# The down products of a SwiGLU block: 26 products of 256 columns replaced by 49 products of 128

## The chip, the cores and the metric

The kernel runs on one core of one Trainium2 chip. Its time is the device time of one execution in microseconds (us). A core has five engines with instruction streams of their own: PE (TensorE, the matmuls; its weight loads are shown apart as PEld), DVE (VectorE), ACT (ScalarE), POOL (GpSimd) and SP (SyncE, which here only issues transfers). PE reads its operands from SBUF, the on-chip memory of 128 partitions, and writes PSUM, in banks of 128x512 f32 values. Data moves between SBUF and DRAM by DMA.

## The reference

Two blocks follow each other, everything in f32:

```
attention, for 8 batches x 8 heads, 576 positions, 64 wide:
    ret = (q @ k.T) / 8 * decay(head)        # lower triangle, gamma ** distance
    x   = ret @ v                            # bridged to 4608 tokens x 512
feed-forward:
    g   = x @ w_gate                         # 512 -> 1536
    val = x @ w_val                          # 512 -> 1536
    out = (silu(g) * val) @ w_out            # 1536 -> 512
```

The weights arrive as 64-bit values and are rounded to f32 on the chip.

## The kernel before, in words

**Tiles and stages.** The 4608 tokens are worked through as a first tile of 512 and four tiles of 1024 (in the code `n` = 1 to 4). Each tile has an up stage (gate and value) and a down stage (the product with w_out). The first tile is plain: `up0` and `down0` use 512-column matmuls, and while they run the attention of the first heads is computed and the weights are rounded (by ACT and DVE). From then on the attention of the head pairs that a later tile needs is spread as small pieces ("ticks" and `pieces`) between the matmuls of the tile before; `go_on(3)` places three such pieces behind a product of a down stage.

**The instruction streams.** The order on each engine is the order in which the program emits instructions (a manual schedule); `later(at, f)`, tables of slots and `merge` decide it. Waits on semaphores are added where data or a buffer is needed.

**Up stages** of the 1024-token tiles use a seven-product scheme (Strassen's, in a variant with fewer sums) at two levels. Weight sums for it come from DRAM (`up_sets`, written during tile 1), sums of x are made on POOL and DVE. The matmuls are those of L1183 with 256 moving columns; results are read from PSUM on DVE and ACT (L1040, L1197), and POOL multiplies silu by val into `hid` (L1198).

**Down stages before.** `hid` holds 4 hidden groups x 4 token blocks of 256 tokens, each with 3 pieces of 128 hidden features (`qd`), so one operand is 128 x 3 x 256 = 128x768 values. The output has two halves of 256 columns. The plain form would need 4 x 4 x 2 = 32 block products; the table `DOWN` needs 26. Each of its lines names the PSUM accumulator, the operand slot, the operand sums made just before ("hops", in place in `hid` and in four more slots `hsum`), and the readings of the accumulator into eight partial results `part`. A product is 3 x 2 f32 matmuls (L1378); each f32 matmul is two passes on PE, so 12 passes of 256 moving columns. In `down_step` the hops go to POOL in one step of three (L886), else to DVE (L886, or L881 for a negated sum). An accumulator is read as 128x512 on DVE (L1040) or copied by ACT; sums of partial results without an accumulator are on POOL (L1040). Four PSUM banks are used in rotation.

**Weight sums of the down stages.** While the first tile's last up steps and its `down0` run, `out_sums` makes the sums of w_out that `DOWN` needs (`OUT_SUMS`): for `qd` 0 and 1 on POOL, for `qd` 2 on DVE (L886, 128x256). ACT first negates four blocks (`negate`, L916) so that POOL needs no negated sums. Each operand is stored to DRAM (`dn_ops`, 26 of 128x768) by SP's queue in 78 transfers of 128 KB. In the down stages `fetch` brings them back into a ring of eight places of 128x768, through ACT's queue and, for some, SP's. The first tile's outputs are copied from PSUM by ACT into `part[4:8]` (`out0`, L869), which the weight sums of `qd` 2 also use, and stored from there.

**The last steps of a down stage** also hold sums of x for the next tile's up stage (`x_first`, on POOL and DVE).

Of the kernel before, what the change touches and what calls it, by code (L numbers as in the profile page):

```python
# [22 lines left out]
def tables(gamma, scale, L):  # L23
# [27 lines left out]
DOWN = [  # L51
    "0= | 1: sub 16 1 11 | copy 0",
    "1= | 11: add 3 3 2, add 3 3 11, sub 17 7 3 | copy 1",
    "2= | 2: nad 3 3 15 | copy 2",
    "1+ | 16: nad 7 7 16 | copy 3",
    "3= | 17: sub 18 0 17 | sub 3 3 b",
    "2+ | 3: add 11 11 8, nad 11 11 9 | add 1 b 1",
    "0+ | 7: sub 9 5 9, sub 1 1 9, sub 13 13 1 | sub 3 3 b",
    "3+ | 18: sub 19 8 13, sub 12 12 19, add 0 0 2 | copy 4",
    "1+ | 11: add 16 4 12, add 3 6 16 | copy 5",  # L60
    "2= | 13: sub 16 17 16 | sub 2 b 2",
    "3+ | 0: nad 9 15 0 | sub 6 2 b",
    "0= | 3:  | copy 7",
    "1= | 16: add 12 12 0 | sub 7 7 b",
    "3+ | 9:  | add 1 b 1, neg 7 1",
    "2+ | 5: add 13 13 10 | copy 8",
    "1+ | 12:  | sub 6 6 b",
    "0= | 19:  | sub 6 6 b, out 4 6",
    "2= | 13: sub 7 1 10 | sub 2 b 2, sub 2 2 7",
    "3+ | 15: add 3 3 14, nad 3 3 15 | add 3 b 3, out 3 3",  # L70
    "1= | 6: add 8 8 1 | sub 7 b 7",
    "2+ | 7:  | copy 9",
    "3+ | 3: sub 14 14 13 | add 9 b 9",
    "0+ | 8: add 4 4 6, sub 4 8 4 | add 5 b 5, sub 0 0 5, sub 8 5 8, out 5 8",
    "2+ | 10:  | add 0 b 0, sub 7 b 7, out 1 0, sub 4 4 7, sub 9 7 9, out 2 9",
    "3+ | 14:  | add 2 b 2, out 6 2",
    "0+ | 4:  | add 4 b 4, out 0 4",
]
OUT_SUMS = [
    "14 | 10: add 8 4 5, add 9 2 3, nad 10 8 9",  # L80
    "2 | 11: add 11 0 1",
    "9 | 5: ",
    "19 | 9: neg 9 9",
    "15 | 12: sub 12 3 7",
    "0 | 11: sub 11 11 8",
    "1 | 13: sub 13 1 5",
    "6 | 10: add 10 0 2",
    "3 | 12: add 9 2 8, sub 12 1 9",
    "22 | 9: add 9 9 7",
    "4 | 11: sub 11 0 3",  # L90
    "11 | 13: nad 13 3 6",
    "7 | 0: ",
    "25 | 10: sub 10 6 2",
    "20 | 8: add 12 6 7, add 8 8 12",
    "23 | 4: ",
    "16 | 9: nad 9 5 7",
    "8 | 11: add 11 2 4",
    "5 | 13: add 13 1 3",
    "18 | 10: sub 10 12 13",
    "10 | 8: sub 13 7 13, sub 8 13 0",  # L100
    "17 | 9: add 9 5 12",
    "24 | 12: ",
    "12 | 3: ",
    "13 | 13: ",
    "21 | 6: ",
]


# [4 lines left out]
def terms(text):  # L113

    return [t.split() for t in text.split(",") if t.strip()]


def lines(table):

    r = []  # L120
    for line in table:
        f = [s.strip() for s in line.split("|")]
        e = [int(f[0][0]), f[0][1] == "="]
        for s in f[1:-1]:
            slot, ops = s.split(":")
            e += [int(slot), terms(ops)]
        r.append(e + [terms(f[-1])])
    return r
# [3 lines left out]
def kernel(  # L132
# [37 lines left out]
    P = 128  # L170
# [59 lines left out]
    hsum = rest[:, dn_at + 4096 : dn_at + 4096 + 3072].rearrange("p (s q x) -> p s q x", s=4, q=NQ)  # L230
# [636 lines left out]
    def out0():  # L867
        for i, (bank, o) in enumerate(zip(banks, part[4:8], strict=True)):
            nc.scalar.copy(out=o, in_=bank)  # L869
            nc.sync.dma_start(out=out[i * P : (i + 1) * P, :], in_=o)  # L870


    down = lines(DOWN)
    N = len(down)

    def add(eng, op, view, to=None):
        dst, srcs = view(int(op[1])) if to is None else to, [view(int(a)) for a in op[2:]]
        if op[0] == "neg":
            eng.tensor_scalar(out=dst, in0=srcs[0], scalar1=-1.0, scalar2=None, op0=ALU.mult)
        elif op[0] == "nad" and eng is nc.vector:  # L880
            eng.scalar_tensor_tensor(out=dst, in0=srcs[0], scalar=-1.0, in1=srcs[1], op0=ALU.mult, op1=ALU.subtract)  # L881
        elif op[0] == "nad":
            eng.tensor_tensor(out=dst, in0=srcs[0], in1=srcs[1], op=ALU.add)
            eng.tensor_scalar(out=dst, in0=dst, scalar1=-1.0, scalar2=None, op0=ALU.mult)
        else:
            eng.tensor_tensor(out=dst, in0=srcs[0], in1=srcs[1], op=ALU.add if op[0] == "add" else ALU.subtract)  # L886

    up_sets = [[dr.tile([P, 1792], F32, name=f"up{qd}_{o}") for o in SETS] for qd in range(NQ)]
    dn_ops = [dr.tile([P, 768], F32, name=f"dn{i}") for i in range(N)]
# [6 lines left out]
    vector_places = x0_places + more_places[6:] + [rest[:, part_at + TB * i : part_at + TB * (i + 1)] for i in range(8)]  # L896

    def events_of(text):
        r = []
        for line in text:  # L900
            i, s = line.split("|")
            slot, ops = s.split(":")
            r += [(int(op[1]), op) for op in terms(ops)] + [(None, int(slot), int(i))]
        return r

    swaps = {"add 9 2 3, nad 10 8 9": "sub 9 14 2, sub 10 9 8", "neg 9 9": "", "nad 13 3 6": "sub 13 14 6", "nad 9 5 7": "sub 9 15 7"}
    signed = list(OUT_SUMS)
    for old, new in swaps.items():
        at = [i for i, line in enumerate(signed) if old in line]
        assert len(at) == 1  # L910
        signed[at[0]] = signed[at[0]].replace(old, new)
    negatives = [x_odd[:, r, 640 : 640 + TB] for r in (2, 3)] + more_places[4:6]

    def negate(qd):
        for n, s in enumerate((3, 5)):
            nc.scalar.mul(out=negatives[2 * qd + n], in_=w_dn[:, qd, s // 2, s % 2], mul=-1.0)  # L916

    def out_sums(qd):


        place = {}

        def free(p):
            if not any(p is q for q in x0_places):
                sum_places.append(p)

        eng, sum_places = (nc.vector, vector_places) if qd + 1 == NQ else (nc.gpsimd, pool_places)
        events = events_of(OUT_SUMS if qd + 1 == NQ else signed)

        def view(s):  # L930
            if s > 13:
                return negatives[2 * qd + s - 14]
            return w_dn[:, qd, s // 2, s % 2] if s < 8 else place[s]

        def used(e):
            return [e[1]] if e[0] is None else [int(a) for a in e[1][2:]]

        def release(k):

            for s in list(place):  # L940
                for e in events[k + 1 :]:
                    if s in used(e):
                        break
                    if s == e[0]:
                        free(place.pop(s))
                        break
                else:
                    free(place.pop(s))

        def do(k):  # L950
            e = events[k]
            if e[0] is None:
                _, slot, i = e
                nc.sync.dma_start(out=dn_ops[i][:, qd * TB : (qd + 1) * TB], in_=view(slot))
            else:
                new = sum_places.pop(0)
# [605 lines left out]
```

## Time and profile before

Three runs took 1024.98, 1025.04 and 1025.64 us (median 1025.04). The profile is that of one execution of 1026.62 us, whose span on the core is 1024.9 us; 1.7 us lie around the span.

| | busy, us | share of the span |
|---|---|---|
| PE | 1003.7 | 98% |
| PEld | 823.0 | 80% |
| DVE | 713.3 | 70% |
| POOL | 557.5 | 54% |
| ACT | 286.3 | 28% |

The four down stages lie at 328.7 to 406.0, 547.6 to 622.6, 757.5 to 826.8 and 953.6 to 1021.1 us of the span, 289.1 us together. The first holds the most attention work, the last none. The granted clock of TensorE is 1.00 in all four.

How to read the lines: a line of the timeline is start, duration (us), engine, code line, operation, output<-inputs, shapes and a count when several of one kind ran in a row; in square brackets stands how long the engine had been idle and what ended it. A line of the groups ends with the busy time, the mean of one in ns, and the idle time before them. Names like bankB are PSUM banks; arena, rest and io are parts of SBUF; dn is the DRAM copy of the down weight sums.

### The profile page before, as it was taken

Reading aid. Unit: us, or ns where it says so; the run is one execution under the profiler, and the core shown is the slowest. Engines: PE = TensorE matmul, PEld = TensorE weight load, DVE = VectorE, ACT = ScalarE, POOL = GpSimd, SP = SyncE. Lnnn points to the kernel's source line nnn. Section 1 sums busy time; section 2 is a strip of 40 time slices with the busy share of each in tenths; the row PEclk is TensorE's granted clock in tenths of the full one; section 3 lists DMA queues with packets and bytes.
Section 4 is the critical chain, followed back from the end, with each engine's and each line's share of the span. In section 5 each row is a group of like instructions: output and inputs, shape, how many; then the busy total and the mean of one; then the engine's idle time right before and its main releaser. Section 6 shows DMA issues by size and latency. Waiting matters only on the chain.

```text
span 1024.9 us, 21387 instructions
## 1 busy us (share of the span) xinstructions
PE 1003.7 (98%) x8336; PEld 823.0 (80%) x8336; DVE 713.3 (70%) x1215; ACT 286.3 (28%) x638; POOL 557.5 (54%) x602
## 2 busy tenths in 40 slices
PE   6999989899999999999999999999999999999998
PEld 5654545788888888888888888888888888888887
DVE  5488877588787766876778688848585767566644
ACT  4465531122332411132332111133320012232110
POOL 3400178997563208665656247755582486566515
PEclk9999999999999999999999999999999999999999
DMA  9999877966496897656658767444455454445552
GB/s 244 253 272 239 202 203 247 275 202 176 120 266 157 221 238 225 194 157 174 187 181 225 195 186 210 148 141 144 157 193 155 144 185 154 143 147 188 175 161 100
DMA packets 281612, 194.38 MB, mean 190 GB/s; under 512 B 212968, under 2 KB 251112, under 8 KB 281512
## 3 DMA queue, kind: packets, MB, share of 16 engines
q1 hardware_dynamic: 247112, 93.52, 35.6%
q10 hardware_dynamic: 33760, 99.10, 29.5%
q8 instruction: 66, 1.08, 0.4%
q0 software_dynamic: 640, 0.39, 0.2%
q14 instruction: 34, 0.28, 0.1%
HBM read 154.04 MB, written 38.93 MB: 188 GB/s over the span
## 4 chain that ended last, share of the span: by engine, by line
PE 69%; DVE 2%; issue 1%; SPq 0%; DMA 0%; DVEq 0%; ACT 0%
PE bankC L1183 9%; PE bankB L1183 9%; PE bankA L1183 9%; PE bankE L1183 9%; PE bankB L1378 7%; PE bankE L1378 7%; PE bankC L1378 7%; PE bankA L1378 6%; PE outer L1183 2%; PE inner L1183 2%; DVE rest L1040 2%; PE outer L532 1%; PE outer L559 1%; PE inner L573 1%; PE inner L543 1%
## 5 line engine op out<-in xcount | busy, mean ns | idle before, releaser
L1040 POOL TENSOR_TENSOR rest<-rest 128x512 f32<-128x512 f32 (+1 forms) x141 | 150.3, 1077 | 156.1 <-DVE rest L1040 114.1
L1198 POOL TENSOR_TENSOR arena<-rest,io 128x256 f32<-128x256 f32 x156 | 113.8, 740 | 88.6 <-ACT io L1197 83.2
L1197 ACT ACTIVATE io<-rest 128x256 f32<-128x256 f32 x192 | 79.4, 417 | 212.0 <-DVE rest L1040 149.6
L1183 PE MATMUL bankB<-rest,arena 128*128 128x256 f32 x448 | 114.9, 381 | 1.0 <-DVE rest L1040 0.9
L1040 DVE TENSOR_TENSOR rest<-bankB,rest 128x512 f32<-128x512 f32 x116 | 78.5, 685 | 47.7 <-PE bankB L1183 32.2
L1183 PE MATMUL bankA<-rest,arena 128*128 128x256 f32 x412 | 105.4, 381 | 1.4 <-POOL rest L1040 0.9
L1183 PE MATMUL bankC<-rest,arena 128*128 128x256 f32 x416 | 106.4, 380 | 0.4 <-DVE rest L1040 0.2
L1040 DVE TENSOR_TENSOR rest<-bankA,rest 128x512 f32<-128x512 f32 x110 | 74.5, 684 | 45.9 <-PE bankA L1183 21.3
L1040 DVE TENSOR_TENSOR rest<-bankC,rest 128x512 f32<-128x512 f32 x110 | 74.7, 685 | 32.0 <-PE bankC L1183 18.9
L1183 PEld LDWEIGHTS bankB<-rest,arena 128*128 128x128 f32 x448 | 84.5, 190 | 13.8 <-POOL rest L1040 1.2
L1183 PE MATMUL bankE<-rest,arena 128*128 128x256 f32 x372 | 95.0, 380 | 0.4 <-DVE rest L1040 0.3
L1040 DVE TENSOR_TENSOR rest<-bankE,rest 128x512 f32<-128x512 f32 x106 | 71.8, 685 | 31.3 <-PE bankE L1183 14.8
L1183 PEld LDWEIGHTS bankA<-rest,arena 128*128 128x128 f32 x412 | 77.7, 190 | 13.6 <-DVE rest L1040 1.8
L1183 PEld LDWEIGHTS bankC<-rest,arena 128*128 128x128 f32 x416 | 78.3, 190 | 12.6 <-DVE rest L1040 1.4
L1040 POOL TENSOR_TENSOR arena<-arena 128x256 f32<-128x256 f32 (+1 forms) x80 | 74.4, 953 | 12.1 <-DMA up<-arena 6.2
L1183 PEld LDWEIGHTS bankE<-rest,arena 128*128 128x128 f32 x372 | 69.9, 190 | 11.7 <-DVE rest L1040 1.6
L886 POOL TENSOR_TENSOR rest<-rest 128x256 f32<-128x256 f32 x43 | 33.4, 800 | 53.8 <-DVE rest L407 36.6
L1378 PE MATMUL bankB<-arena 128*128 128x256 f32 x264 | 61.0, 381 | 0.0
L1378 PE MATMUL bankE<-arena 128*128 128x256 f32 x264 | 60.8, 380 | 0.0
L1378 PEld LDWEIGHTS bankE<-arena 128*128 128x128 f32 x264 | 49.9, 190 | 6.9
L1378 PEld LDWEIGHTS bankB<-arena 128*128 128x128 f32 x264 | 49.8, 190 | 6.9
L886 POOL TENSOR_TENSOR arena<-arena 128x768 f32<-128x768 f32 x24 | 47.0, 1961 | 15.3 <-DVE arena L1198 14.7
(267 smaller groups left out, 1881.1 us busy)
## 6 DMA issues: line engine op xcount, KB each, us to landing
arena<-up ACTq DMA_DIRECT2D x63, 896.0 KB, 4.6
arena<-dn ACTq DMA_DIRECT2D x65, 384.0 KB, 3.5
arena<-dn SPq DMA_DIRECT2D x39, 384.0 KB, 3.2
dn<-rest SPq DMA_DIRECT2D x78, 128.0 KB, 2.0
out_dram<-rest SPq DMA_DIRECT2D x35, 256.0 KB, 3.1
qk<-in_q_dram SPq DMA_DIRECT2D x108, 72.0 KB, 3.1
qk<-in_k_dram SPq DMA_DIRECT2D x108, 72.0 KB, 3.1
up<-arena SPq DMA_DIRECT2D x14, 512.0 KB, 2.9
```

The lines of the kernel that those rows point to most:

```text
L532: m = nc.tensor.matmul(value(i, hl, c), s["v"][rows, at], ret[rows, c % 2 if whole(i) else hl, c // 2], start=start, stop=start, skip_grou ...
L543: nc.tensor.matmul(z[half[hl], r, c], s["kn"][chunk(i, hl, 2 * c + r)], s["v"][rows, at], start=True, stop=True, skip_group_check=True)
L559: nc.tensor.matmul(xr[half[hl]] if c + 1 == NC else value(i, hl, c), state[half[hl], c, :], s["qT"][half[hl], ts(c, L)], start=False, stop ...
L573: nc.tensor.matmul(sc[chunk(i, hl, 2 * c + r)[0], r if whole(i) else hl, c], kT[half[hl], at], qT[half[hl], at], start=True, stop=True, sk ...
L886: eng.tensor_tensor(out=dst, in0=srcs[0], in1=srcs[1], op=ALU.add if op[0] == "add" else ALU.subtract)
L1040: eng.tensor_tensor(out=out, in0=a, in1=b, op=ALU.add if sign > 0 else ALU.subtract)
L1183: m = nc.tensor.matmul(b[:, g * TB : (g + 1) * TB], w[:, g], x, start=(opens and g == 0), stop=True, skip_group_check=True)
L1197: nc.scalar.activation(out=s, in_=src[:, 0:TB], func=AF.Silu)
L1198: (nc.vector if busy and o != 2 else nc.gpsimd).tensor_tensor(out=hid[:, qd, 2 * H + h, 2 * T + t], in0=src[:, TB : 2 * TB], in1=s, op=ALU ...
L1378: nc.tensor.matmul(b[:, m * TB : (m + 1) * TB], lhs[:, qd, ts(m, P)], w[:, qd], start=(opens and qd == 0 and m == 0), stop=(qd == NQ - 1), ...
```

## The change

The change replaces the down stages of the four 1024-token tiles and the weight sums that feed them; the up stages, the attention and the first tile's matmuls stay.

- **Products.** The down product is cut into 4 token blocks x 4 hidden groups x 4 output quarters of 128 columns, 64 plain block products, and the seven-product scheme is used at two levels, which needs 49. `DOWN_SETS` gives the seven outer products, `down_slots` the order of the 49 slots; the last two products of a set (7 and 4) are woven into the next set. A slot is 2 x 3 f32 matmuls, 12 passes of 128 moving columns. An accumulator is 128x256, still four banks in rotation.
- **Operand sums** (`down_sums`). The outer sums combine whole blocks of `hid`: 16 of 128x768 on DVE per tile, at slots 1, 3, 5, 7 (set 5), 8 to 11 (set 7), 14 to 17 (set 6) and 24 to 27 (set 3). The inner sums are four for each of seven sets, 28 of 128x768 on POOL per tile: the first three of set 1 are put into the last slots of the up stage, the fourth at slot 0, the others at slots 1-4, 6-9, 13-16, 20-23, 27-30 and 34-37. Before, a tile had 18 sums on DVE and 10 on POOL.
- **Readings** (`read`, `takes`). Accumulators are read as 128x256: 55 on DVE and 8 copies on ACT in each tile; sets 6 and 5 are read twice. POOL has two 128x512 sums (`closed`).
- **Fetches.** A transfer of 128x768 now holds two products' operands: 24 of 384 KB and one of 192 KB a tile, in the same ring, and `go_on(1 + s % 2)` places three attention pieces per two slots.
- **Weight sums** (`sums_of_w`, `out_sums`). 44 sums of 128x256 on POOL (`qd` 0 and 1 together) and 44 of 128x128 on DVE (`qd` 2); 80 stores of them and 9 of unchanged blocks (`raw_stores`) on SP's queue. The negations on ACT are gone. `out0` copies into `hid0[0]`, `hid0[2]` and the two halves of `io` instead of `part[4:8]`.
- **The rest.** `x_first` has its sums every other slot over the last 10 or 18 slots, and the four ticks of tile 1 are put in front of slots 4, 14, 26 and 38.

```diff
+DOWN_SETS = (1, 2, 4, 7, 6, 5, 3)
+def down_slots():
+    slots, begins = [], []
+    for k in range(len(DOWN_SETS)):
+        begins.append(len(slots))
+        own = [(k, i) for i in (1, 5, 2, 6, 3)]
+        if k:
+            own[1:1], own[5:5] = [(k - 1, 7)], [(k - 1, 4)]
+        slots += own
+    return slots + [(k, 7), (k, 4)], begins
+def sums_of_w():
+    r = []
+    def inner(o):
+        z = lambda k, m: (o, k, m)
+        t = lambda j: (o, j)
+        kept = [(o, 1, z(0, 0)), (o, 2, z(1, 0)), (o, 3, z(1, 1))] if o > 3 else []
+        r.append([(t(1), z(0, 1), z(0, 0)), (t(3), z(1, 1), z(0, 1)), (t(2), z(1, 1), t(1)), (t(4), z(1, 0), t(2)), *kept,
+                  (o, 5, t(1)), (o, 7, t(3)), (o, 6, t(2)), (o, 4, t(4))])
+    def outer(o, a, b):
+        r.append([((o, k, m), (a, k, m), (b, k, m)) for k in range(2) for m in range(2)])
+    for o in (1, 2, 3):
+        inner(o)
+    for o, a, b in ((7, 3, 0), (5, 0, 1), (6, 3, 5), (4, 2, 6)):
+        outer(o, a, b)
+        inner(o)
+    return r
...
-        for i, (bank, o) in enumerate(zip(banks, part[4:8], strict=True)):
+        for i, (bank, o) in enumerate(zip(banks, (hid0[0], hid0[2], io[:, 0:512], io[:, 512:1024]), strict=True)):
             nc.scalar.copy(out=o, in_=bank)
             nc.sync.dma_start(out=out[i * P : (i + 1) * P, :], in_=o)
...
-    def negate(qd):
-        for n, s in enumerate((3, 5)):
-            nc.scalar.mul(out=negatives[2 * qd + n], in_=w_dn[:, qd, s // 2, s % 2], mul=-1.0)
...
+        for f, at in zip(down_sums(n)[1](0, nc.gpsimd)[:3], (begins[-3] + 6, begins[-2] + 6, begins[-1] + 6), strict=True):
+            later(at, f)
...
-    def down_step(n, i):
-        label, opens, slot, hops, ops = down[i]
-        for op in hops:
-            add(nc.gpsimd if i % 3 == 1 and op[0] != "nad" else nc.vector, op, hid_view)
...
+    def down_sums(n):
+        quarter = {1: (0, 0), 2: (0, 1), 7: (1, 0), 4: (1, 1), 6: (0, 0), 3: (0, 1)}
...
+        def outer(o, eng):
+            a, b, sign = {5: (7, 4, 1), 7: (1, 7, -1), 6: (5, 1, -1), 3: (2, 6, -1)}[o]
+            return [lambda k=k, t=t: combine(eng, block(o, k, t), block(a, k, t), block(b, k, t), sign)
+                    for k, t in ((0, 1), (1, 1), (0, 0), (1, 0))]
+        def inner(j, eng):
+            a, (s1, s2, s4, s3) = (lambda k, t: block(DOWN_SETS[j], k, t)), spots[j]
+            return [lambda: combine(eng, s1, a(0, 1), a(1, 1), 1),
+                    lambda: combine(eng, s2, s1, a(0, 0), -1),
+                    lambda: combine(eng, s4, a(1, 0), s2, -1),
+                    lambda: combine(eng, s3, a(0, 0), a(0, 1), -1)]
...
+    def down_stage(n):
+        outer, inner, left = down_sums(n)
...
+        for o, at in {5: 1, 7: 8, 6: 14, 3: 24}.items():
+            for j, f in enumerate(outer(o, nc.vector)):
+                later(at + j * (2 if o == 5 else 1), f)
+        later(0, inner(0, nc.gpsimd)[3])
+        for j, at in {1: 1, 2: 6, 3: 13, 4: 20, 5: 27, 6: 34}.items():
+            for m, f in enumerate(inner(j, nc.gpsimd)):
+                later(at + m, f)
...
+        def takes(o):
+            return {1: [(held, None)], 2: [(one, held)], 4: [(two, None)], 7: [(kept, held)], 6: [(held, held), (kept, kept)],
+                    5: [(held, held), (three, kept)], 3: [(held, held)]}[o]
+        def read(o, c, b, first):
+            src = b[:, 0:TB].rearrange("p (m x) -> p m x", m=2)
+            for dst, base in takes(o):
+                if first and base is None:
+                    nc.scalar.copy(out=at_corner(dst, c), in_=src)
+                else:
+                    combine(nc.vector, at_corner(dst, c), src, at_corner(base if first else dst, c), 1)
...
+        def go(s):
...
+            for f in after.pop(s, ()):
+                f()
...
+            for m in range(2):
+                for qd in range(NQ):
+                    nc.tensor.matmul(b[:, ts(m, P)], lhs[:, qd, ts(m, P)], w[:, qd],
+                                     start=(opens and m == 0 and qd == 0), stop=(qd == NQ - 1), skip_group_check=True)
...
+            after_tick()
+            read(o, {1: 11, 5: 22, 6: 12, 4: 21, 2: 11, 3: 12, 7: 22}[i], b, i in (1, 5, 6, 4))
...
+            go_on(1 + s % 2)
```

## Prediction

> **What bounds the kernel now.** I read the page's busy table first, then the table of stretches of time for the four down stages, then single lines of the timeline and the groups.
>
> ```profile
> PE 1003.7 (98%) x8336; PEld 823.0 (80%) x8336; DVE 713.3 (70%) x1215; ACT 286.3 (28%) x638; POOL 557.5 (54%) x602
> ```
> ```profile
> 328.70:406.00 77.30, 77.30 (x861) 67.52 (x861) 53.32 (x86) 20.47 (x58) 27.50 (x19) 1.00 0.82 219
> 547.60:622.60 75.00, 75.00 (x730) 65.61 (x728) 54.87 (x106) 10.39 (x22) 31.23 (x21) 1.00 0.74 194
> 757.50:826.80 69.30, 69.21 (x387) 60.63 (x382) 46.13 (x59) 6.18 (x11) 34.50 (x21) 1.00 0.51 160
> 953.60:1021.10 67.50, 67.50 (x313) 59.09 (x311) 34.18 (x38) 6.94 (x13) 29.57 (x19) 1.00 0.46 144
> ```
>
> Each row is a down stage: its length, then the busy time of PE, PEld, DVE, ACT and POOL (us), the granted clock, the DMA share and GB/s. PE is busy from end to end and nothing makes it wait; POOL is at 36 to 50%, DVE at 51 to 73%. So the time is PE's, and any wait that the new sums cause is new time. The clock is full, so fewer columns are less time.
>
> **1. The matmuls.** The pace of a down product:
>
> ```profile
> 331.44 2.59 PE bankC L1378 x12
> ```
> ```profile
> 20.76 0.60 PE L466 MATMUL bankE<-ident,rest 128*128 128x128 f32 x4
> ```
> ```profile
> 336.21 0.19 PEld L1378 LDWEIGHTS bankE<-arena 128*128 128x128 f32 x1
> 336.32 0.19 PEld L1378 LDWEIGHTS bankE<-arena 128*128 128x128 f32 x1
> ```
>
> The first line is from the chain of waits: 12 passes of 256 columns in 2.59 us, 0.2158 us each. Removed: 4 tiles x 26 x 12 = 1248 passes x 0.2158 = 269.3 us. The change adds 4 x 49 x 12 = 2352 passes of 128 columns. No such stream exists before; the nearest row are the transposes of the second line, four matmuls of 128 columns with a weight load each: the group's mean is 272 ns, so (0.60 - 0.272) / 3 = 0.109 us from one to the next. The two loads of the third excerpt start 0.11 us apart, so a load need not hold a pace of 0.109 up, though one is recorded as 0.19 us long. I take 0.109: 2352 x 0.109 = 256.4 us, **-12.9 us**. Each ns of pace is 2.35 us. Bounds: 0.108 (half of 0.2158), -15.3 us, and 0.190 if recorded loads did not overlap, +178 us. I keep the far end for a rival, since the load pair and the transposes stand against it.
>
> [...]
>
> **2. The weight sums and the end of the first tile.**
>
> ```profile
> 135.83 0.72 ACT L916 ACTIVATE rest<-rest 128x256 f32<-128x256 f32 x2 [11.63 <-DMA dn<-rest]
> 143.23 0.27 PE L567 MATMUL outer<-qT,kT 64*64 64x64 f32 x2 [1.55 <-DVE kT L492]
> 181.45 0.59 ACT L869 COPY rest<-bankE 128x512 f32<-128x512 f32 x1 [3.58 <-DMA dn<-rest]
> 182.09 1.13 PE L1183 MATMUL bankE<-x_odd,arena 128*128 128x256 f32 x4 [0.93 <-ACT rest L869]
> ```
>
> ACT's negations waited 11.63 us for stores; behind them stood copies of the attention, then DVE, then PE (0.95 us at 139.33 and the 1.55 us shown). The copies of out0 waited for stores from the same places, and PE 0.93 us for them. The negations go and out0 gets other places, so these waits go: 0.95 + 1.55 + 0.93 = -3.4 us. What is late next: SP issues 89 stores in place of 78, at about 0.40 us each (50.9 us for the 78 between 127.4 and 178.3), +4.4 us on its queue, and the loads of later heads stand behind them. On POOL 44 sums of 128x256 replace 46 (no change). On DVE 44 sums of 128x128 replace 24 of 128x256: no row shows the width, so between half of 0.42 us and the 0.89 us of a 256-wide sum beside POOL: from 44 x 0.21 - 24 x 0.89 = -12 us to 44 x 0.89 - 24 x 0.42 = +29 us on DVE, which idles elsewhere in that stretch (a wait of 6.86 us for ACT). I take -2.5 us, between -3.4 and +3, near the shown waits because the cover is idle DVE time.
>
> **3. The operand sums.** A tile had 18 sums of 128x768 on DVE and 10 on POOL; it gets 16 and 28. What they cost beside each other:
>
> ```profile
> 990.67 0.95 DVE L886 TENSOR_TENSOR arena<-arena 128x768 f32<-128x768 f32 x1
> ...
> 1001.27 1.92 POOL L1040 TENSOR_TENSOR rest<-rest 128x512 f32<-128x512 f32 x1 [22.65 <-DVE rest L1040]
> ...
> 1002.09 1.91 DVE L881 SCALAR_TENSOR_TENSOR arena<-arena 128x768 f32<-128x768 f32 x1
> 1003.15 6.79 POOL L886 TENSOR_TENSOR arena<-arena 128x768 f32<-128x768 f32 x3
> ...
> 1005.68 0.69 DVE L1040 TENSOR_TENSOR rest<-bankE,rest 128x512 f32<-128x512 f32 x1 [1.08 <-POOL arena L886]
> ...
> 1006.28 1.97 DVE L886 TENSOR_TENSOR arena<-arena 128x768 f32<-128x768 f32 x1
> ```
> ```profile
> 142.38 4.87 POOL L886 TENSOR_TENSOR rest<-rest 128x256 f32<-128x256 f32 x6
> 143.11 3.56 DVE L886 TENSOR_TENSOR rest<-rest 128x256 f32<-128x256 f32 x4
> ```
>
> A sum takes DVE 0.95 us alone and 1.97 us while POOL adds; POOL's 1.81 us alone become 2.26. Readings from PSUM keep their 0.69 us. So sums of SBUF operands on the two engines take turns. At 256 columns a pair in turn takes 0.89 us (3.56 / 4), where alone they take 0.42 + 0.73: 0.26 to 0.28 overlap. For 768 a pair in turn thus takes 0.95 + 1.81 - 0.28 = 2.48 us.
>
> The last tile, which has no attention: a slot is 12 x 0.109 = 1.308 us, and a bank is needed again four slots after its product, so a reading may be three slots (3.92 us) late. DVE's readings stand in its queue behind the outer sums. In slots 5 to 17 ten outer sums take turns with POOL: 24.8 us, where 13 slots last 17.0. Laid out in order, the outer sums end at 2.5, 5.3, 9.5 and 12.0 us from the stage's start (set 5), 14.5, 17.0, 19.4, 21.9 (set 7), 24.4, 26.8, 29.3, 31.8 (set 6). The reading of slot 9 then ends at 17.4 where slot 13 wants the bank at 17.0 (+0.4), that of slot 11 at 22.3 against 20.0 (+2.3 with the first), that of slot 17 at 32.2 against 30.2 (+2.0): 4.7 us. The four sums at slots 24 to 27 add 0.5. POOL begins late: in the last 13 us of the up stage it was busy 10.7, and three moved sums (5.4 us) do not fit ahead of the last multiplies of L1198 that make the stage's operands; the fourth sum of set 1 ends at about 8.7 us, slot 6 wants it at 7.85, and later POOL sums keep pace (2.47 us against two slots, 2.6): +1. In all **+6.3 us**.
>
> The others add to this. DVE's other work in the stages (sums of durations, in which the down operations are taken off) is 25.0, 29.8 and 15.1 us in tiles 1 to 3, and PE's attention 9.9, 7.6 and 1.9 us, the lengths above 67.4. Tile 3: one attention tick in early slots, 5.9 us of DVE into some 3 us of idle time, less 1.9 of PE, and the sums of x at the end, +1.5 over the last tile: 7.8. Tile 2: of its attention 18/49 falls in the first 18 slots, 9.4 us of DVE, less 3 idle and 2.8 of PE, +3.6; +2 more in slots 18 to 27; 12. Tile 1: 17.75 us of attention, of it 6 us in those slots, but 9.9 us of PE beside it and POOL idle before the stage: 5.7. Sum of the stalls **+31.8 us**. Bounds: 0 if readings always come in time, and 52 if DVE is bound in tiles 1 to 3 by every outer sum taking 2.48 us (92.4, 87.6 and 77.7 us against 71.7, 74.1 and 66.1 for PE: +20.7, +13.5, +11.6 in the order of tiles 2, 1, 3) with 6.3 in tile 4.
>
> **Hidden edits.** Readings are 55 x 0.42 + 8 x 0.37 of ACT a tile and stand in the sums above; ACT, at 10 to 27% in the stages, covers its copies, and if not they cost 8 x 0.37 = 3 us a tile. The fetches have the same bytes in 100 transfers for 104, at a DMA share of 0.46 to 0.82; a late one would cost its 3.5 us of landing (DMA issues of the page). The ticks of tile 1 and the sums of x keep their times (two slots last 2.62 us where a step lasted 2.59). The last add is of half the width, 0.2 us less at most.
>
> **Sum.** The profiled execution is 1026.62 us (span 1024.9 + 1.7), 1.6 us or 0.15% above the median. -12.9 - 2.5 + 31.8 = +16.4 us, so on the median 1025.0 + 16.4 = **1041 us**; the stages come to 79.8, 83.7, 73.9 and 70.4 us.
>
> **The rivals.**
> - *Faster, the turns hidden.* If POOL yields at the end of each sum so that DVE waits less than three slots everywhere, stalls are near 0: 1025.0 - 15.4 = 1010 us. For it: the stages before have 28 such sums and no idle PE. Against: the sums' time alone is 65.9 us a tile (16 x 0.95 + 28 x 1.81) for 35.2, and ten outer ones stand close together. It decides if the stalls stay under 15.4 us.
> - *No change*: stalls of 13 to 17 us, 1025.
> - *The turns are the bound*: POOL's 28 sums, the sums of x and the attention fill the stages of tiles 1 to 3: +52 instead of +31.8, 1062 (1055 to 1070).
> - *Loads are not hidden in a stream of 128 columns*: at the mean of 0.109 and 0.190, a pace of 0.15, the stream is 352.8 us, +83.5, with most stalls hidden in the slower slots: 1025.0 + 83.5 - 2.5 = 1106 us. [...]
>
> **How the numbers follow.** Chances: forecast (1023 to 1053) 0.62, faster 0.16, no change 0.04, turns as bound 0.12, loads 0.06. A measurement here can tell about 0.2%, 2 us. So faster 0.16, same 0.04, slower 0.80. The range 1013 to 1063 leaves out the loads (0.06), about half of the faster case, which spreads around 1010, and a third of the bound. The forecast's own range, 1027 to 1053, is stalls of 17 to 43 us.
>
> **What would show it.** Passes of L1378's successor at 0.109 us; no L916 and no store ahead of L869; DVE sums of 128x768 near 1.9 us and POOL's near 2.4; PE idle ended by DVE's readings in slots 10 to 21 of each stage, most in tile 2; tile 1 least hurt among those with attention. Wrong if 768-wide sums keep 0.95 us, or if PE waits for weights or for DMA instead.

## The result

The changed kernel took 1066.83 us (median of four, 1064.97 to 1067.42), the kernel before 1025.34 us beside it: a ratio of 1.040, interval 1.038 to 1.042. It is 41.5 us slower. The forecast was 16 us slower, 1041 us; the direction holds, the time lies 4 us above the range and the loss is two and a half times the forecast one.

The page's table of busy times of the changed kernel, and from its page the shares of the chain that ended last, by engine:

```profile
PE 1014.7 (95%) x9440; PEld 860.6 (81%) x9440; DVE 781.3 (73%) x1375; ACT 274.7 (26%) x626; POOL 690.2 (65%) x660
...
PE 55%; DVE 10%; issue 3%; DMA 3%; SPq 1%; ACT 0%; POOL 0%; DVEq 0%; ACTq 0%
```

PE went from 98% of the span to 95%; DVE now holds 10% of the chain, where it held 2%. The stretches of the profile of the changed kernel, columns as before (length, busy PE, PEld, DVE, ACT, POOL, clock, DMA share, GB/s): all up to the first 1024-token down stage, then down stage, up stage, down stage and so on.

```profile
0.00:334.30 334.30, 315.93 (x3217) 222.58 (x3218) 236.18 (x469) 123.46 (x270) 175.78 (x224) 0.99 0.80 216
334.30:415.70 81.40, 76.88 (x1137) 75.28 (x1136) 64.55 (x122) 17.52 (x56) 61.56 (x39) 1.00 0.74 197
415.70:564.10 148.40, 142.89 (x1269) 122.46 (x1268) 105.64 (x190) 42.39 (x94) 86.72 (x97) 0.99 0.61 182
564.10:647.30 83.20, 77.60 (x1006) 74.94 (x1004) 72.18 (x141) 7.68 (x20) 64.19 (x41) 0.98 0.65 165
647.30:787.20 139.90, 136.81 (x996) 118.43 (x996) 95.95 (x162) 39.95 (x88) 86.59 (x98) 0.99 0.46 158
787.20:859.80 72.60, 69.93 (x663) 69.04 (x658) 63.88 (x93) 3.35 (x9) 68.88 (x39) 0.98 0.45 143
859.80:986.60 126.80, 126.80 (x590) 111.61 (x589) 83.94 (x128) 36.36 (x79) 84.41 (x95) 1.00 0.45 161
986.60:1061.90 75.30, 67.85 (x589) 66.22 (x587) 58.50 (x73) 4.01 (x11) 62.06 (x33) 1.00 0.40 128
```

Three things are to be seen: POOL's busy time in the down stages doubled (27.5 to 34.5 us before, 61.6 to 68.9 now; this includes time in which an instruction is held up: a 128x768 sum of POOL is recorded as 2.41 us at 994.52, as 1.83 us on the mean in the kernel without DVE's outer sums); the last up stage, 126.8 us, is what it was, but the two before it grew (141.6 to 148.4, and 134.9 to 139.9); and the clock, 1.00 throughout before, is below 1.00 in five rows. The table sets the spans (1065.5 against 1024.9 us) beside the prediction's terms. The pace of a pass is 0.1117 us (1.34 us a product, below), so all products are 2352 x 0.1117 = 262.7 us; stalls are the stages' lengths above that and above the attention (19.8 us: the four stages before, 289.1 us, less the 269.3 us of their products).

| term | predicted, us | measured, us |
|---|---|---|
| products: 269.3 us become | 256.4 (-12.9) | 262.7 (-6.6) |
| stalls in the down stages | +31.8 | +30.0 |
| weight sums, up to tile 1's down stage (328.7 to 334.3) | -2.5 | +5.6 |
| up stages of tiles 2 and 3 (+6.8, +5.0) | 0 | +11.8 |
| sum (the end of the span is 0.2 us shorter) | +16.4 | +40.6 |

The down stages themselves were forecast at 79.8, 83.7, 73.9 and 70.4 us and last 81.4, 83.2, 72.6 and 75.3.

**The products.** From the timeline of the changed kernel:

```profile
405.39 1.50 PE L1364 MATMUL bankA<-arena,rest 128*128 128x128 f32 x12
...
406.73 1.50 PE L1364 MATMUL bankE<-arena 128*128 128x128 f32 x12
```

A product starts every 1.34 us (405.39, 406.73), 12 passes of 0.1117 us. The weight loads, recorded as 0.19 to 0.20 us each on the mean, are hidden in that pace: the rival that they are not has no part in it.

**The turns.** From the timeline of the changed kernel's tile 4, the first operand sums:

```profile
989.56 5.69 DVE L930 TENSOR_TENSOR rest<-arena 128x768 f32<-128x768 f32 x1 [1.29 <-POOL arena L1088]
990.85 3.58 POOL L930 TENSOR_TENSOR rest<-arena 128x768 f32<-128x768 f32 x2
...
994.52 2.41 POOL L930 TENSOR_TENSOR rest<-rest,arena 128x768 f32<-128x768 f32 x1
995.17 0.41 DVE L930 TENSOR_TENSOR rest<-bankA,rest 128x256 f32<-128x256 f32 x1
995.51 2.23 DVE L930 TENSOR_TENSOR rest<-arena 128x768 f32<-128x768 f32 x1
997.00 2.41 POOL L930 TENSOR_TENSOR rest<-arena,rest 128x768 f32<-128x768 f32 x1
997.66 0.41 DVE L930 TENSOR_TENSOR rest<-bankB,rest 128x256 f32<-128x256 f32 x1
998.00 2.23 DVE L930 TENSOR_TENSOR rest<-arena 128x768 f32<-128x768 f32 x1
998.13 1.60 PE L1364 MATMUL bankB<-arena 128*128 128x128 f32 x12 [0.65 <-DVE rest L930]
...
1013.03 1.16 PE L1364 MATMUL bankA<-arena 128*128 128x128 f32 x8 [1.96 <-DVE rest L930]
```

From 995.5 on a DVE sum starts every 2.49 us (995.51, 998.00): the forecast cycle was 2.48. The readings between them keep their 0.41 us. PE waits for DVE's readings at slots 8, 9, 12, 13, 15 (the last line) and 21; the forecast had 13, 15 and 21. What the forecast did not have is the first line: 5.69 us, in which two POOL sums went ahead.

Over the four stages the waits of PE that a reading of DVE ended come to 1.3, 4.6, 2.5 and 7.5 us. The longest wait in tile 1 is of another kind:

```profile
345.13 0.57 PE L533 MATMUL inner<-qT,kT 64*64 64x64 f32 x22 [3.25 <-issue]
```

It stands in the middle of a run of attention matmuls, and the profile shows nothing that PE waited for ("issue"). The kernel before has no such wait there. Of the variants of the changed kernel below, seven have it (2.4 to 3.2 us) and three have not (the one group of weight sums, and those without POOL's or without DVE's sums). Its cause is open.

**Ahead of tile 1's down stage**, first an excerpt of the timeline of the changed kernel, then stretches:

```profile
125.68 6.26 ACTq L242 DMA_DIRECT2D rest<-in_k_dram  x4
...
134.62 0.43 ACTq L247 DMA_DIRECT2D kn<-in_k_dram  x1
...
136.31 0.37 ACT L544 COPY even<-inner 128x256 f32<-128x256 f32 x1 [11.31 <-DMA dn<-rest]
...
139.45 5.56 DVE L930 TENSOR_TENSOR rest<-rest 128x128 f32<-128x128 f32 x8
144.93 0.77 DVE L452 STREAM_TRANSPOSE qT<-qk 128x576 f32<-128x576 f32 x1
145.62 0.73 DVE L452 STREAM_TRANSPOSE kT<-qk 128x576 f32<-128x576 f32 x1
...
146.41 0.37 PE L527 MATMUL outer<-qT,kT 64*64 64x64 f32 x2 [4.85 <-DVE kT L452]
```
```profile
146.50:148.00 1.50, 1.50 (x37) 1.38 (x38) 1.50 (x3) 0.14 (x1) 1.42 (x3) 0.50 1.04 287
148.00:150.00 2.00, 2.00 (x3) 0.84 (x3) 1.97 (x4) 0.23 (x1) 2.00 (x3) 0.50 1.03 288
150.00:152.00 2.00, 2.00 (x3) 0.67 (x2) 2.00 (x6) 0.07 (x1) 0.82 (x2) 0.50 0.69 192
152.00:154.00 2.00, 2.00 (x6) 0.95 (x5) 1.86 (x7) 1.95 (x8) 0.00 (x0) 0.95 0.53 152
```

Eight narrow weight sums stand ahead of the transposes that PE needs; beside POOL they take 5.56 us (0.70 us each; a 256-wide one took 0.89). PE waits 4.85 us, and then the granted clock is 0.50 for 6 us. ACT's wait of 11 us for stores is still there though its negations are gone. Ahead of it on ACT's queue stand loads of k (the first two lines), and the kernel before has the same ones ahead of its negations:

```profile
125.76 6.51 ACTq L282 DMA_DIRECT2D rest<-in_k_dram  x4
...
133.91 0.39 ACTq L287 DMA_DIRECT2D kn<-in_k_dram  x1
```

**In the up stages**, from the timeline of the changed kernel, tile 1's end and tile 2's:

```profile
427.99 0.81 ACTq L915 DMA_DIRECT2D arena<-up  x2
...
432.48 2.04 PE L1073 MATMUL bankB<-rest,arena 128*128 128x256 f32 x4 [3.81 <-DMA arena<-up]
```
```profile
656.27 0.95 SPq L1321 DMA_DIRECT2D out_dram<-rest  x2
...
659.69 0.69 DVE L930 TENSOR_TENSOR rest<-bankB,rest 128x512 f32<-128x512 f32 x1 [4.26 <-DMA out_dram<-rest]
...
660.53 1.78 PE L1073 MATMUL bankB<-rest,arena 128*128 128x256 f32 x4 [2.90 <-DVE rest L930]
```

In the first the third set of up weights is fetched at 428, 12 us after the down stage. In tile 1 the fetch is called behind odd slots only, and the last slot is number 48: with 49 products the call behind the last one is missing. In the second, DVE must not overwrite a partial result before its store has landed, and SP issued that store at 656, behind loads of q, k and v.

### The profile page after: what moved, and what is told of

The parts are those of the page before. It is cut to its first block, busy times and chain, and to the rows that moved or that the text cites. A ratio compares the mean times of both kernels' runs of the same rounds, so it can differ in the third digit from the quotient of the medians.

```text
span 1065.5 us, 23992 instructions
## 1 busy us (share of the span) xinstructions
PE 1014.7 (95%) x9440; PEld 860.6 (81%) x9440; DVE 781.3 (73%) x1375; ACT 274.7 (26%) x626; POOL 690.2 (65%) x660
## 4 chain that ended last, share of the span: by engine, by line
PE 55%; DVE 10%; issue 3%; DMA 3%; SPq 1%; ACT 0%; POOL 0%; DVEq 0%; ACTq 0%
PE bankE L1073 9%; PE bankC L1073 8%; PE bankB L1073 8%; PE bankA L1073 8%; PE bankC L1364 5%; DVE rest L930 4%; PE bankB L1364 4%; PE bankA L1364 4%; PE bankE L1364 3%; DVE arena L930 3%; PE inner L1073 2%; PE outer L1073 2%; DMA arena<-up 1%; PE outer L492 1%; DMA arena<-dn 1%
## 5 line engine op out<-in xcount | busy, mean ns | idle before, releaser
L930 POOL TENSOR_TENSOR rest<-rest 128x256 f32<-128x256 f32 (+1 forms) x173 | 162.8, 955 | 157.5 <-DVE rest L367 58.2
L930 DVE TENSOR_TENSOR rest<-bankC,rest 128x512 f32<-128x512 f32 (+1 forms) x151 | 88.6, 597 | 45.1 <-PE bankC L1073 28.1
L930 DVE TENSOR_TENSOR rest<-bankB,rest 128x512 f32<-128x512 f32 (+1 forms) x143 | 84.0, 595 | 49.9 <-PE bankB L1073 29.9
L930 DVE TENSOR_TENSOR rest<-bankA,rest 128x512 f32<-128x512 f32 (+1 forms) x147 | 85.2, 592 | 43.2 <-PE bankA L1073 33.0
L930 POOL TENSOR_TENSOR rest<-arena 128x768 f32<-128x768 f32 (+1 forms) x58 | 101.2, 1756 | 23.3 <-DVE arena L1088 15.2
L930 DVE TENSOR_TENSOR rest<-bankE,rest 128x512 f32<-128x512 f32 (+1 forms) x145 | 86.5, 601 | 31.9 <-PE bankE L1073 18.3
L930 POOL TENSOR_TENSOR arena<-arena 128x256 f32<-128x256 f32 (+2 forms) x84 | 82.6, 1004 | 12.0 <-DMA up<-arena 6.1
L1073 PEld LDWEIGHTS bankA<-rest,arena 128*128 128x128 f32 x408 | 77.7, 191 | 12.9 <-POOL rest L930 1.9
L930 POOL TENSOR_TENSOR rest<-rest,arena 128x768 f32<-128x768 f32 (+1 forms) x42 | 74.4, 1772 | 21.1 <-ACT rest L1128 14.9
L930 POOL TENSOR_TENSOR rest<-arena,rest 128x768 f32<-128x768 f32 (+1 forms) x38 | 60.2, 1583 | 2.0
L930 DVE TENSOR_TENSOR arena<-arena 128x768 f32<-128x768 f32 x32 | 56.7, 1786 | 0.0
```

Of the source, the lines that this page charges most:

```text
L930: eng.tensor_tensor(out=out, in0=a, in1=b, op=ALU.add if sign > 0 else ALU.subtract)
L1073: m = nc.tensor.matmul(b[:, g * TB : (g + 1) * TB], w[:, g], x, start=(opens and g == 0), stop=True, skip_group_check=True)
```

## The experiments

**One group of weight sums per step, and the orders at the stages' ends.** Two kernels, each the changed one with

```diff
-        for _ in range(min(2, len(last_groups))):
+        for _ in range(min(1, len(last_groups))):
```

> One group of DVE weight sums per step of the first tile's down products instead of two. Theory: PE's wait of 4.85 us at 146.4 us comes from eight sums of 128x128 (5.56 us, each 0.70 beside POOL) that stand ahead of the transposes of the next head pair, and the granted clock of 0.50 for the 6 us after it follows from that wait. Then the wait falls below 2.5 us, the clock stays at 1.00 there, the first 1024-token down stage starts at about 328 instead of 334.3 us, and the kernel takes about 1061 us. Rival: the sums only move on, and stand ahead of a later pair's transposes; the start stays at 333 or later and the kernel at 1066 us.

and with

```diff
-            if n == 1 and s % 2:
+            if n == 1 and (s % 2 or s + 1 == N):
                 fetch(2)
...
-        def whole(a, T, t, d):
+        def whole(a, T, t, d, queue=nc.sync):
...
-                f(nc.sync)
+                f(queue)
...
-            whole({2: one, 5: three, 3: held}[o], 0 if o in (2, 3) else 1, t, 0 if o == 2 else 1)
+            whole({2: one, 5: three, 3: held}[o], 0 if o in (2, 3) else 1, t, 0 if o == 2 else 1, nc.scalar if n + 1 < NTILE and (o, t) in ((5, 1), (3, 0), (3, 1)) else nc.sync)
```

> Two orders at the end of the down stages of tiles 1 and 2 (and 3): the fetch that tile 1 leaves out behind its last, odd product, and the last output stores on ACT's queue instead of SP's. Theory: the wait of 3.81 us at 432.5 us is the up weights fetched too late, that of 2.90 us at 660.5 us is a reading that needs a partial result whose store stood on SP's queue behind loads of q, k and v, and each brings 1.7 us of lost clock. Both go, the two up stages after them are shorter by 5.5 and 4.6 us, the kernel takes about 1057 us. Rival: the sums of x that DVE makes late at the end of the stage hold the up stage up anyway: 1063 to 1066 us.

The first took 1059.6 us (ratio to before 1.031, 1.028 to 1.034). The wait of 4.85 us became one of 1.58, the clock stayed at 1.00 up to the down stage, which began at 331.3 us: half of the way to 328. So the narrow sums are the cause of the long wait and of the lost clock behind it. Over all kernels the down stage begins at 329.0 to 332.7 us with one group per step (four traces) and at 333.3 to 337.1 us with two (seven). Of the 2.6 us that remain, about 0.9 are waits for sums on POOL: 2.10 and 1.46 us at 193 and 200 us, where the kernel before has 0.93, 0.86 and 0.86 us between 182 and 198 us; the rest was not traced. Some 3 us more that this kernel gained lie in later stages that the edit does not touch: tile 4 took 69.9 us for 75.3, tile 3 76.3 for 72.6 (why, see below).

The second took 1056.9 us (1.029, 1.025 to 1.033), as expected: the two up stages lasted 142.7 and 135.0 us, within 1.1 us of before, with the clock at 1.00. The trace has the third set of weights issued at 417 instead of 428 us and the output stores at 638 to 643 instead of 656 us. Both waits and the lost clock behind them come from the two queue orders; the up stage of tile 3 has the store order alone, that of tile 2 has both, and there it is the wait's releaser that points at the fetch.

**Without POOL's sums, and without DVE's.** The inner sums are left out (the products read the blocks), or the outer ones, so neither kernel computes the block; only their times are used, one run of each.

```diff
-                    lambda: combine(eng, s3, a(0, 0), a(0, 1), -1)]
+                    lambda: combine(eng, s3, a(0, 0), a(0, 1), -1)][:0] or [lambda: None] * 4
...
-            return {1: block(o, 0, 0), 2: block(o, 1, 0), 3: s4, 4: block(o, 1, 1), 5: s1, 6: s2, 7: s3}[i]
+            return {1: block(o, 0, 0), 2: block(o, 1, 0), 3: block(o, 1, 0), 4: block(o, 1, 1), 5: block(o, 0, 1), 6: block(o, 1, 1), 7: block(o, 0, 1)}[i]
```

> The 28 inner sums of each tile on POOL are left out, and the products read the blocks themselves; DVE's work is unchanged in number. Theory that sums on DVE and POOL take turns: DVE's sums of 128x768 take 0.95 us, its readings come in time, and the four down stages last about 76, 74, 68 and 66 us (49 products x 1.34 us and the attention) instead of 81.4, 83.2, 72.6 and 75.3; no clock is lost in tiles 2 and 3; the kernel takes about 1037 us. Rival that DVE simply has too many operations: the stages keep their lengths within 2 us each, 1063 us.

```diff
-        for o, at in {5: 1, 7: 8, 6: 14, 3: 24}.items():
-            for j, f in enumerate(outer(o, nc.vector)):
-                later(at + j * (2 if o == 5 else 1), f)
```

> The 16 outer sums of each tile on DVE are left out, and the products read what lies in those places; POOL's 28 sums stay. Theory of turns: POOL's sums take 1.81 us instead of 2.3 and more, DVE's readings come in time, the stages last about 77, 75, 69 and 67 us, the kernel about 1040 us. Rival that POOL's 28 sums are late by themselves (28 x 1.81 = 50.7 us, three of them pushed into the stage from before): PE waits for POOL and the stages stay at 80, 82, 72 and 73 or more, 1058 us or more.

Without the inner sums the stages took 76.4, 75.8, 68.4 and 66.6 us (for 81.4, 83.2, 72.6 and 75.3), without the outer ones 76.5, 77.0, 68.7 and 66.6; the kernels took 1040.9 and 1045.5 us, with the waits outside the down stages still there. The groups of the changed kernel, of the one without inner sums and of the one without outer sums (busy time, mean ns of one, idle before):

```profile
L930 DVE TENSOR_TENSOR arena<-arena 128x768 f32<-128x768 f32 x32 | 56.7, 1786 | 0.0
```
```profile
L930 DVE TENSOR_TENSOR arena<-arena 128x768 f32<-128x768 f32 x32 | 29.8, 948 | 0.0
```
```profile
L930 POOL TENSOR_TENSOR rest<-arena,rest 128x768 f32<-128x768 f32 x24 | 44.0, 1835 | 3.1 <-PE bankA L1361 1.7
```

Each engine's sums run at their own speed (0.95 and 1.83 us) as soon as the other has none, and PE then hardly waits (in tile 4 it is busy for 66.1 of 66.6 us in both), with DVE's operations all there in the first kernel and POOL's all there in the second. Neither engine is too full by itself; the stalls are what they cost each other. (In tile 1 3.25 of the 5 us gained are the wait without a shown cause, which neither kernel has.)

**Smaller operations on one side.** Either engine's 768-wide sums are made as three of 256, in one run each. Both kernels call this in place of `combine`, the second without `sign`:

```diff
+            def by(out, x, y, sign):
+                for q in range(NQ):
+                    combine(eng, out[:, q], x[:, q], y[:, q], sign)
```

> Each inner sum of 128x768 on POOL is made as three of 128x256 (84 a tile instead of 28), DVE unchanged. If the two engines take turns operation by operation, a DVE sum waits for the rest of 0.73 us at most and takes 1.3 to 1.6 us instead of 1.75 to 2.3; POOL now needs 28 x 3 x 0.73 = 61 us of turns and DVE 15, more than the 65.7 us that the products last, so POOL's sums come late and waits of PE end with POOL, not DVE; tile 4 lasts 71 to 76 us. If they only share a bandwidth, DVE's sums stay at 1.75 to 2.3 us and the stages keep their lengths.

> Each outer sum of 128x768 on DVE is made as three of 128x256 (48 a tile instead of 16), POOL unchanged. Turns operation by operation: each third waits for a whole POOL sum, so it takes 1.5 to 2.0 us, an outer sum 5 us and more, and the readings behind it come later; tile 4 lasts over 78 us and the kernel over 1080 us. Shared bandwidth: a third takes 0.7 to 0.9 us, an outer sum about 2.5 us, tile 4 stays at 70 to 76 us and the kernel within 5 us of 1067.

With POOL's sums in thirds the kernel took 1107.9 us, the stages 84.4, 96.3, 86.2 and 83.6 us, more than either theory gave, and PE's longest wait in tile 4 ended with DVE, not with POOL. Its timeline at the start of tile 4, the engines DVE and POOL:

```profile
1022.28 20.54 DVE L930 TENSOR_TENSOR rest<-arena 128x768 f32<-128x768 f32 x1 [1.84 <-POOL arena L1088]
1023.58 4.15 POOL L930 TENSOR_TENSOR rest<-arena 128x256 f32<-128x256 f32 x6
1027.67 2.09 POOL L930 TENSOR_TENSOR rest<-rest,arena 128x256 f32<-128x256 f32 x3
...
1039.91 2.09 POOL L930 TENSOR_TENSOR rest<-arena 128x256 f32<-128x256 f32 x3
1042.74 0.41 DVE L930 TENSOR_TENSOR rest<-bankA,rest 128x256 f32<-128x256 f32 x1
```

One DVE sum of 0.95 us waited while 27 POOL sums passed it, until POOL itself had to wait for PE. PE stood for 15 us. Beside each other the two engines' sums hold each other up (2.49 us a pair in the changed kernel, 0.95 and 1.83 us apart), but not in turns of one each: of the later sums of the same stage the first five took 0.94 or 0.95 us, while POOL stood, and those beside POOL about 1.1 to 1.5 us, about what the theory of turns gave; this one took 20.54. The 5.69 us in the changed kernel's tile 4 is the same thing in small. It also explains why two tiles changed places between kernels: tile 3 and tile 4 lasted 72.6 and 75.3 us in the changed kernel, where the first sum of the tile took 1.00 and 5.69 us, and 76.3 or 76.2 and 69.9 us in the kernels with the one group and with the fetch and store orders, which leave these stages as they are; there it took 5.21 or 5.22 and 1.46 or 1.47.

With DVE's sums in thirds the kernel took 1106.0 us and the stages 92.3, 91.6, 83.1 and 82.7 us, as the theory of turns expected; while POOL was adding, three thirds took 5.58 us (1.86 each). The largest group of thirds has a mean of 0.72 us: in it are stretches in which POOL itself waited for DVE's sums, and there three took 1.08 us. For a shared bandwidth the expectation gave tile 4 70 to 76 us, and it took 82.7.

Readings from PSUM are not held up: one took 0.41 us inside a POOL sum (997.66, in the changed kernel's tile 4) and 0.41 us where POOL stood (1042.74 above). Nor does the sum that starts first go first: the record of the one of 20.54 us begins at 1022.28, those of the 27 at 1023.58 and later.

**The outer sums spread.** Every other slot has one, instead of runs of four.

```diff
-        for o, at in {5: 1, 7: 8, 6: 14, 3: 24}.items():
+        for o, at in {5: 1, 7: 8, 6: 15, 3: 24}.items():
             for j, f in enumerate(outer(o, nc.vector)):
-                later(at + j * (2 if o == 5 else 1), f)
+                later(at + 2 * j, f)
```

> The 16 outer sums of a tile stand at every other slot (1-7, 8-14, 15-21, 24-30) instead of in runs of four; number and sizes unchanged. Theory: a turn of DVE and POOL together takes 2.48 us and two slots last 2.68, so DVE keeps up, its readings are under three slots late; tile 4 lasts 67 to 68 us, tile 3 about 70, tiles 1 and 2 about 79 each, the kernel about 1050 us. Rival: it is the amount of turns in a stage and not their bunching, so the four stages sum to 308 or more (312.5 in the changed kernel), 1062 us or more.

> The spread outer sums, the one group of weight sums per step, the fetch and the store order together. If the four causes are apart, their gains add: 1067 less 3.0 at the start of tile 1, less 5.7 and 4.9 in the up stages, less the spread's gain (16 by the theory) gives about 1036 us. If they hide each other, 1045 or more. Under 1025 it would beat the kernel before, which the theory does not give.

Spread alone: 1060.6 us (1.032, 1.029 to 1.035), 6 us less than the changed kernel where the theory gave 16; stages 83.4, 83.0, 68.4 and 68.8, together 303.6 us, between the theory and its rival. Tiles 3 and 4 lie within 1.6 us of the theory. In tile 3 it is the bunching that costs: the first sum took 1.0 us in both kernels, and the stage fell from 72.6 to 68.4 us. In tile 4 most of the gain is the first sum's luck: it took 1.47 us, and the bunched order had 69.9 us with that. In tiles 1 and 2, which have the most attention, spreading gained nothing (tile 1 also lost 3.4 us of clock in that trace). With the three other edits: 1044.3 us (1.017, 1.014 to 1.020), better than the changed kernel by 22 us and still slower than the kernel before; 8 us are missing to the expected sum, most of them in tiles 1 and 2 (6.4 us over the 79 expected of each). Stretches of that kernel, in the order of the table above:

```profile
332.70:413.40 80.70, 76.48 (x1137) 75.12 (x1136) 67.56 (x122) 17.47 (x56) 59.60 (x38) 1.00 0.77 201
413.40:555.80 142.40, 140.99 (x1269) 121.52 (x1268) 105.10 (x190) 42.27 (x94) 86.70 (x98) 1.00 0.66 187
555.80:639.50 83.70, 77.58 (x1006) 75.06 (x1004) 75.48 (x141) 7.68 (x20) 63.88 (x41) 0.98 0.66 169
...
774.40:842.80 68.40, 67.80 (x663) 67.25 (x658) 61.12 (x93) 3.35 (x9) 67.46 (x37) 1.00 0.47 145
```

In tile 2 DVE is busy for 75.5 of 83.7 us. Without POOL's inner sums the same number of DVE's operations took 59.7 us there, so some 16 us are waiting inside its sums.

**Attention moved, and the first sum moved**, both on top of that kernel:

```diff
-        cut = (done + upto + (n == 1) * 2) // 2
+        cut = (done + upto + 2) // 2 if n == 1 else upto
```

> On top of the kernel with the spread sums, the one group, the fetch and the store order: the attention that tiles 2 and 3 had in their down stages is done in the up stages before them. Theory: with the turns spread, what is left over the bare products in tile 2 is DVE's attention work in a stage in which DVE waits for POOL; then the stage falls from 83.7 to 67 to 70 us (it loses 7.6 us of PE's attention too), the up stage before it grows from 142.4 to about 150, tile 3 loses about 1.5 us and its up stage gains 2; the kernel takes about 1037 us instead of 1044. Rival: the up stage has no room either (POOL 61%, DVE 74% there), grows by over 12 us, and the kernel stays at 1043 or more.

```diff
-                later(at + 2 * j, f)
+                later(at + 2 * j, f if (o, j) != (5, 0) else outer(5, nc.gpsimd)[0])
```

> Same kernel with the spread sums and the three orders; only the first outer sum of each tile is made by POOL instead of DVE. In tile 2 this sum took DVE 4.70 us (two POOL sums went ahead of it), PE then waited 2.32 us and the clock fell for 5 us (1.7 us lost). Theory: with that sum in POOL's own order nobody loses a turn there; the wait of 2.3 us early in tile 2 and the lost clock go, the stage falls by 3 to 4 us to about 80, the others stay within 1 us. Rival: the next sum on DVE loses the turns instead, and the wait stays over 2 us.

With the attention moved, tile 2's down stage fell from 83.7 to 71.9 us, but the up stage before it grew from 142.4 to 156.3 and that of tile 3 from 134.9 to 138.0; the kernel took 1050.5 us (1.024, 1.022 to 1.025). The rival holds: the attention is cheaper where it is. (The place at which it writes the next x among the stage's reads changes too, and it does not compute the block, so only the times of this kernel are used.) With the first sum on POOL tile 2 fell to 80.4 us with the clock at 1.00, as expected, but in tiles 3 and 4 the next sum lost the turns (3.34 and 5.79 us) and these stages grew by 0.8 us each. Tile 1 took 83.4 us for 80.7, with the clock at 0.96, which was not expected either. 1042.0 us in a single run. What would make DVE win its turn was not found.

**One part of the change in the kernel before.**

```diff
-        for i, (bank, o) in enumerate(zip(banks, part[4:8], strict=True)):
+        for i, (bank, o) in enumerate(zip(banks, (hid0[0], hid0[2], io[:, 0:512], io[:, 512:1024]), strict=True)):
```

> The kernel before with one part of the change alone: the first tile's outputs are copied into two blocks of the first tile's hidden values and the two halves of io, not into part[4:8]. Prediction's reading: the copies' wait of 3.58 us for stores of weight sums goes, and with it PE's wait of 0.93 us at 182 us; the kernel takes 1024.1 us instead of 1025.0, within what can be told. Rival: PE's next wait, for POOL's sums of x at 188 us, grows by as much, no change.

A ratio of 0.9994, 0.9979 to 1.0008: no change. PE's wait of 0.93 us at 182 us is gone, and the two behind it grew from 0.86 and 0.86 us (one ended by DVE, one by POOL) to 1.55 and 1.48 us, both ended by POOL's sums. So part of what PE waits for POOL in the changed kernel is this wait, moved on.

## Why the prediction was right and wrong

- **The operand sums (step 3)** were right in mechanism: the cycle of a pair 2.49 us for 2.48, PE waiting for DVE's readings at the three slots named, and taking out either side's sums ends it. That the sum came to +30.0 us for +31.8 is in part luck. By tile the stalls were about 5.8, 9.9, 4.9 and 9.4 us for 5.7, 12, 7.8 and 6.3; of tile 1's, 3.25 us are the wait that no reading ended, and 3.4 us of tiles 2 and 3 are lost clock that the step did not have. Tile 4 was 3.1 us over by the one sum that lost two turns; without that it took 69.9 us in two traces, for 70.4. Waits for readings were to be the most in tile 2 and the stalls least in tile 1; they were the most in tile 4 and least in tile 3.
- **The products (step 1)** were mis-sized: 0.1117 us for 0.109, 6.3 us over four tiles. The four transposes gave (0.60 - 0.272) / 3, which with 0.60 rounded to 10 ns is 0.108 to 0.111, and every ns counts 2352 times; the step took a pace from three gaps of another kind of matmul as if it were exact. The loads (0.19 to 0.20 us each) are hidden in the pace.
- **The weight sums (step 2)** had the wrong sign: -2.5 forecast, +5.6 measured, outside its own ends (-3.4 to +3). It gave the 11.6 us wait of ACT to the negations, because they were the instruction that the wait ended in. With the negations gone another ACT instruction ended the same wait (11.31 us), and even with one group per step PE's two waits of 0.95 and 1.55 us are there, at 0.83 and 1.58 us. As the traces read, ACT's queue was held by loads of k that needed places from which weight sums were still being stored; no run moved these loads. It put the end of +29 us of DVE time for the narrow sums down as covered, by idle time that lies elsewhere; at the tick, eight of them stood in front of the transposes. And the wait of out0 was only the first of three: taking it away moved it on. (The step's 0.40 us per store on SP's queue does not follow from its 50.9 us for 78, which is 0.65 us.)
- **The hidden edits** named a price of 3.5 us for a late fetch and gave it no place. The step looked at bytes and transfers, not at where the call stands: an odd number of products dropped the last call in tile 1. The output stores' place on SP's queue behind the loads was not looked at either. Together 11.8 us, put at nothing in the sum, of which putting both right gave back 10.6. PE's wait of 3.81 us for DMA is also one of the signs that the prediction named for being wrong.
- **The lost clock** stands in no step. Over two-microsecond stretches the clock below 1.00 adds up to 10.2 us (one less the clock, times the stretch): 3.4 at the wait at 146 (0.3 of it before the wait ended), and 1.7 each after the waits at 432, 577, 660 and 809 us; it is part of the terms above. So these five waits, of 2 to 5 us, cost PE 1.7 to 3.4 us more than themselves.
- The rival of turns as the bound in every tile was priced at 1062 us; the kernel took that long for other reasons, since the stages stayed near the forecast.
- Two slips changed nothing: the forecast's lower end is 1023 in one sentence and 1027 in another (17 us of stalls give 1027), and ACT is at 9, not 10, to 27% in the stages.

## What to carry to other kernels

Sums of two SBUF operands on DVE and POOL were one resource here (128x768 values: 0.95 and 1.83 us apart, 2.49 us a pair beside each other): add their times on both engines stage by stage, spread them, and do not expect an order between them. Replacing a stage by one with another count of steps moves every call that hangs on the step's number (a fetch, a store, a group of sums), so lay the first and last steps of each stage out queue by queue. Where PE will wait in one piece as long as the five waits of 1.96 to 4.85 us here, add the clock that it may lose behind it (1.7 to 3.4 us behind each of these, none behind three others of 1.72 to 3.25 us).

## What was not expected of the hardware

- A DVE sum can wait for many POOL sums in a row: 20.54 us with 27 sums of 0.69 us, 5.69 us with two of 1.8 us.
- Waits of PE of 1.96 (809 us), 2.33, 2.90, 3.81 and 4.85 us were followed by a granted clock of 0.50 for some 3 to 6 us; waits of 3.25 us (345 us), 1.96 us (1013 us) and 1.72 us (1023 us) were not, the clock staying at 1.00. The length alone does not decide: the same wait of 2.10 us for POOL, at 191 to 199 us, was followed by lost clock in the kernel with all four edits and in the one with the first sum on POOL, and not in those with the one group, with the fetch and store orders, and with the spread sums alone. What does stays open.
